# Moving the first sequence's last transposes, and two units of its filter stage, in a Fourier-filter plus SwiGLU kernel

## The chip, the cores and the metric

The kernel runs on one core of a Trainium2 chip. The metric is device microseconds of one execution. Executions are listed as fast or slow; all those used here were fast. The engines are PE (TensorE), VectorE (DVE in the profile), ScalarE (ACT), GpSimd (POOL), and SyncE (SP), which issues most DMAs. "L437" is line 437 of that kernel's own source; the changed kernel is two lines longer, so its later lines differ by one to three.

## The reference, cut to what matters

```python
# x: (8, 3008, 256);  filt_r, filt_i: (1505, 256);  d_ff = 1536
X = np.fft.rfft(x, axis=1)
y = np.fft.irfft(X * (filt_r + 1j * filt_i)[None], n=3008, axis=1)
x = y.reshape(24064, 256)
rms = np.sqrt(np.mean(x * x, axis=-1, keepdims=True) + 1e-06)
xn = x / rms * rms_g
g, val = xn @ w_gate, xn @ w_val
out = (g * sigmoid(g) * val) @ w_out
```

The transform over 3008 = 47 x 64 points is done as two short transforms by matmul, the filter between them, and back. The feed-forward then takes the result in 48 tiles (6 for each of 8 sequences) of 12 slots each. A slot is four gate and value matmuls (`gv`) and four output matmuls (`down`), about 1.3 us of PE. The transforms of the next sequence run between the slots of this one. Only the first sequence has nothing to hide behind: its filter and transposes are a prologue of some 50 us.

## The kernel before

The filter stage of the first sequence. Unit `i` covers two of 32 frequency groups: two matmuls (`b_mm`), two multiplies with the filter (`b_unit`), and the inverse matmuls (`bit_unit`). GpSimd takes four of the units, by way of a copy `v` that ScalarE makes, since the products lie in PSUM, which GpSimd cannot access (the Trainium skill, "Trainium Kernel Development and Optimization", Key Constraints; the trace agrees in that each of its units follows such a copy, of 0.60 us).

```python
eng = nc.vector
if (i in (5, 8, 11, 14)) if b else (i in (3, 7, 10, 13)):
    eng = nc.gpsimd
    v = yp.tile([P, 2, 512], FP32, tag="y", name="v")
    ...
    nc.scalar.activation(out=v, in_=ps, func=AXT.Copy)
    ps = v
eng.tensor_tensor(out=s1, in0=ps, in1=f1, op=ALU.mult)
eng.tensor_tensor(out=s2, in0=ps, in1=f2, op=ALU.mult)
```

`t1_unit(g)` transposes tile `g` of the first transform and evacuates it (VectorE, or ScalarE for `g` 1 and 4). `t2_unit(j, eng, bank)` transposes the `j`-th of twelve pieces after the inverse matmuls; `eng` is 1 for an evacuation by VectorE, 0 for ScalarE. `f_dup` copies half a filter table. `warm_up(n)` and `keep_warm(n)` issue matmuls whose result nobody reads, of 512 and 128 columns; the text calls them dummies. Some lines are joined here, and the comments are added.

```python
t1_unit(0); t1_unit(1)
ps0 = [b_mm(0, i) for i in range(4)]
t1_unit(2); t1_unit(3)
f_dup(0, 0, A)
... # 16 units; then the last inverse blocks
for i in range(12, 16):
    bit_unit(i)
    if i % 2 == 0: keep_warm(4)
warm_up(2, 0)
t2_unit(0, 1); t2_unit(1, 0)
warm_up(2, 0)
first = n_first()          # psn: first tile; squares on ScalarE
warm_up(4, 0)
y_first(*first, 1)
q_unit(0, 0)               # psq; u on VectorE; rho on GpSimd
warm_up(3, 0)
y_first(*first, 0)
scale_split(0, 0)          # hl: rho as two f16 parts, on VectorE
t2_unit(2, 0); t2_unit(3, 0)
warm_up(3, 0)
scale_apply(0, 0, 3)       # psr on PE; xn = y * psr on VectorE
warm_up(1, 0)
t2_unit(4, 0); t2_unit(5, 0)
... # the feed-forward; slots 0 to 5 hold t2_unit(6) to (11)
```

Every later tile but two gets its scale another way. GpSimd computes `rho`, stores it to DRAM (`r_tmp`), SyncE loads it back as a row broadcast to all partitions (`rb`), and GpSimd multiplies: `xn_unit`. The steps are planned by slot:

```python
def norm_plan(b, m, s0, s1, r):
    ...
    steps = (q_unit, rho_load, xn_unit)
    if halved(b, m):                      # late tiles: GpSimd first folds the squares
        at(s1 + 2, fold_unit, b, m)
        r = (4, 8, 11)
    ...
    for d, fn in zip(r, steps):
        at(s1 + d, fn, b, m, ...)
```

In these traces each engine takes up its instructions in program order: in the trace of after, shown below, `hl` waits 1.01 us behind an evacuation although its input is ready.

## Time and profile before

| | before |
|---|---|
| time, median of three | 900.11 us (899.17 to 901.25) |
| span of the profiled execution | 896.9 us |
| PE busy | 877.4 us (98%) |
| first transposes after the inverse (`pt` from `gT`) | 42.37 us |
| first scaling multiply (`xn`) | 48.11 us |
| first output evacuation (`o`, feed-forward tile 0) | 73.57 us |

The page of the profile of before, its busy line and the chain that ended last:

```profile
PE 877.4 (98%) x6307; PEld 563.0 (63%) x6307; DVE 676.7 (75%) x1085; ACT 624.0 (70%) x1063; POOL 427.2 (48%) x384
...
PE 87%; issue 5%; DVE 3%; DMA 2%; POOL 2%; ACT 1%; POOLq 0%; DVEq 0%; ACTq 0%; SPq 0%
```

After the prologue PE is the limit. What a change of the prologue is worth must be read in the prologue's timeline. Three views of before follow, each with start, duration, engine, line, operation and tiles; the bracket is the idle time of the engine before it and what ended it. First VectorE, 18 to 26 us, around the start of the multiplies:

```profile
19.73 0.69 DVE L545 COPY t<-pt 96x1024 f16<-96x1024 f16 x1 [0.75 <-PE pt L543]
22.46 1.29 DVE L545 COPY t<-pt 96x1024 f16<-96x1024 f16 x2 [2.04 <-PE pt L543]
23.66 0.68 DVE L265 TENSOR_TENSOR ss<-psb,fr 128x512 f16<-128x512 f32 x1
```

Then ScalarE in the same time:

```profile
20.25 1.02 ACT L547 ACTIVATE t<-pt 96x1024 f16<-96x1024 f16 x1 [1.70 <-PE pt L543]
21.30 1.94 ACT L510 ACTIVATE fr<-fr 64x2048 f32<-64x2048 f32 x1
```

VectorE idles 2.04 us. The bracket names PE: its transposes of tile 2 (from 21.76 us) stand behind matmuls that need tile 1, which ScalarE evacuates until 21.27. ScalarE then copies the filter half that unit 0 reads, until 23.24. From 23.66 us VectorE multiplies without a gap to 39.88 us. Then the scale chain, all engines, of before:

```profile
42.37 0.86 PE L582 MATMUL pt<-tb,gT 128*128 128x128 f16 x8
...
45.99 1.05 POOL L355 TENSOR_TENSOR rho<-u,mhalf 128x4 f32<-128x4 f32 x1 [1.11 <-DVE u L353]
...
47.08 0.17 DVE L391 CAST hl<-rho 128x4 f16<-128x4 f32 x1 [0.51 <-POOL rho L355]
...
48.11 1.29 DVE L405 TENSOR_TENSOR xn<-psr,y 128x512 f16<-128x512 f32 x2 [0.66 <-PE psr L401]
```

`hl` starts 0.04 us after `rho` ends (45.99 + 1.05 = 47.04): nothing stands between them.

### The profile page before, as it was taken

The page shows a single profiled execution, that of the slowest core. Times are in us where ns is not written, and L with a number is a line of the kernel's source. Part 1 is how long each engine was busy: PE and PEld are TensorE (multiplying, and loading weights), DVE is VectorE, ACT ScalarE, POOL GpSimd, SP SyncE. Part 2 cuts the span into 40 slices and gives each one's busy share as a digit, 9 for nine tenths or more (in the row PEclk, how much of TensorE's full clock was granted, in tenths as well). Part 3 has the DMA queues.
Part 4 walks back from the last instruction along what each step waited for, and adds up shares of the span by engine and source line. Part 5 has one row for each costly group of instructions (what it writes and reads, how often), then busy time and mean ns, then how long its engine had stood idle before and what let it go on. Part 6 is the DMA issues. An engine that isn't in the chain of part 4 may idle for free.

```text
span 896.9 us, 17537 instructions
## 1 busy us (share of the span) xinstructions
PE 877.4 (98%) x6307; PEld 563.0 (63%) x6307; DVE 676.7 (75%) x1085; ACT 624.0 (70%) x1063; POOL 427.2 (48%) x384
## 2 busy tenths in 40 slices
PE   8899999999999999999999999999999999999997
PEld 5666666566666666666666666666666666666556
DVE  6866667788988787888788886887878887555555
ACT  7777666677777766877668766787657765676544
POOL 7842730555635661577326662376515662155300
PEclk9999999999999999999999999999999999999999
DMA  8495725674564337434554347242262232222301
GB/s 200 101 192 169 158 57 185 148 172 103 139 170 115 88 86 202 107 95 114 135 149 105 94 92 196 71 109 82 83 176 72 66 85 56 93 66 48 72 24 48
DMA packets 80094, 101.43 MB, mean 113 GB/s; under 512 B 8108, under 2 KB 56684, under 8 KB 79560
## 3 DMA queue, kind: packets, MB, share of 16 engines
q1 hardware_dynamic: 69688, 84.23, 34.3%
q0 software_dynamic: 10240, 15.96, 11.0%
q8 instruction: 49, 0.80, 0.4%
q14 instruction: 37, 0.30, 0.1%
q10 hardware_dynamic: 80, 0.13, 0.1%
HBM read 67.67 MB, written 46.78 MB: 128 GB/s over the span
## 4 chain that ended last, share of the span: by engine, by line
PE 87%; issue 5%; DVE 3%; DMA 2%; POOL 2%; ACT 1%; POOLq 0%; DVEq 0%; ACTq 0%; SPq 0%
PE po L456 25%; PE pg L437 25%; PE pv L437 25%; PE psi L288 3%; PE psb L238 3%; PE psn L320 2%; PE psa L203 2%; DMA xc<-in_x_dram 1%; DMA rb<-r_tmp 1%; DVE o L463 1%; PE psq L349 1%; DVE hh L442 1%; PE pt L543 0%; POOL xc L188 0%; PE pt L582 0%
## 5 line engine op out<-in xcount | busy, mean ns | idle before, releaser
L442 DVE TENSOR_TENSOR hh<-pv,sg 128x512 f16<-128x512 f32 (+2 forms) x588 | 393.3, 670 | 198.1 <-ACT sg L441 85.8
L441 ACT ACTIVATE sg<-pg 128x512 f16<-128x512 f32 (+2 forms) x588 | 340.8, 580 | 226.5 <-PE pg L437 217.5
L456 PE MATMUL po<-wo,hh 128*128 128x256 f16 x2244 | 342.9, 272 | 2.3 <-DVE o L463 1.6
L437 PE MATMUL pg<-xn,wg 128*128 128x512 f16 (+2 forms) x1176 | 339.5, 370 | 0.2 <-DVE xn L405 0.2
L437 PE MATMUL pv<-xn,wv 128*128 128x512 f16 (+2 forms) x1176 | 339.5, 370 | 0.0
L456 PEld LDWEIGHTS <-hh 128*128 128x128 f16 x2256 | 216.4, 98 | 96.8 <-issue 3.5
L279 POOL TENSOR_TENSOR s<-s,s 128x512 f16<-128x512 f16 x96 | 111.0, 1156 | 230.4 <-DVE s L273 158.3
L437 PEld LDWEIGHTS <-wv 128*128 128x128 f16 x1176 | 114.9, 98 | 129.1 <-issue 0.5
L416 POOL TENSOR_TENSOR xn<-y,rb 128x1024 f16<-128x1024 f32 (+1 forms) x45 | 126.2, 2805 | 42.6 <-DMA rb<-r_tmp 36.2
L437 PEld LDWEIGHTS <-wg 128*128 128x128 f16 x1176 | 111.3, 98 | 12.7 <-issue 0.3
L355 POOL TENSOR_TENSOR rho<-u,mhalf 128x4 f32<-128x4 f32 (+1 forms) x48 | 48.9, 1019 | 68.3 <-DVE u L353 68.0
L293 ACT ACTIVATE t<-psi 96x512 f16<-96x512 f32 x112 | 66.3, 592 | 11.7 <-PE psi L288 6.6
L326 ACT ACTIVATE y<-psn,gsb 128x512 f32<-128x512 f32 (+1 forms) x94 | 63.8, 678 | 9.4 <-PE psn L320 2.4
L273 DVE TENSOR_TENSOR s<-psb,fi 64x512 f16<-64x512 f32 x96 | 65.7, 684 | 3.0
L275 DVE SCALAR_TENSOR_TENSOR s<-psb,fi 64x512 f16<-64x512 f32 x96 | 66.5, 693 | 1.3
L249 DVE TENSOR_TENSOR s<-psb,fr 128x512 f16<-128x512 f32 x96 | 65.4, 681 | 0.0
L340 POOL TENSOR_TENSOR sq<-sq 128x512 f16<-128x512 f16 (+1 forms) x34 | 38.4, 1130 | 36.1 <-ACT sq L332 36.1
L332 ACT ACTIVATE sq<-psn 128x512 f16<-128x512 f32 (+1 forms) x94 | 54.8, 583 | 0.0
L208 ACT ACTIVATE t<-psa 128x512 f16<-128x512 f32 x70 | 41.8, 597 | 5.6 <-PE psa L203 2.4
L288 PE MATMUL psi<-s,wi 128*128 128x256 f16 x248 | 45.4, 273 | 0.0
L238 PE MATMUL psb<-t,wb 96*128 96x256 f16 x224 | 43.0, 272 | 0.9 <-DVE s L266 0.9
L288 PEld LDWEIGHTS <-wi 128*128 128x128 f16 x248 | 24.2, 98 | 27.1 <-issue 2.0
(106 smaller groups left out, 543.7 us busy)
## 6 DMA issues: line engine op xcount, KB each, us to landing
out_dram<-o SPq DMA_DIRECT2D x83, 256.0 KB
xc<-in_x_dram POOLq DMA_DIRECT2D x56, 192.0 KB, 6.0
z_tmp<-t SPq DMA_DIRECT2D x28, 384.0 KB
t<-z_tmp SPq DMA_DIRECT2D x28, 384.0 KB
g_tmp<-t SPq DMA_DIRECT2D x56, 192.0 KB
rb<-r_tmp SPq DMA_DIRECT2D x41, 256.0 KB
t<-g_tmp SPq DMA_DIRECT2D x21, 384.0 KB
t<-g_tmp SPq DMA_DIRECT2D x7, 320.0 KB
```

Source lines behind the costliest of these rows:

```text
L238: nc.tensor.matmul(ps[:, u, :], w[:, k, :], t, start=True, stop=True)
L249: nc.vector.tensor_tensor(out=s1, in0=ps, in1=f1, op=ALU.mult)
L273: nc.vector.tensor_tensor(out=s2[a], in0=ps[e], in1=f2[e], op=ALU.mult)
L275: nc.vector.scalar_tensor_tensor(out=s2[a], in0=ps[e], scalar=-1.0, in1=f2[e], op0=ALU.mult, op1=ALU.mult)
L279: nc.gpsimd.tensor_tensor(out=s, in0=s1, in1=s2, op=ALU.add)
L288: nc.tensor.matmul(ps[:, u, :], wi_at(q, 2 * i + u), ss[q][:, u, :], start=(q == 0), stop=(q == n - 1))
L293: nc.scalar.activation(out=st[b]["t3"][c][:, 2 * r:2 * r + 2, :], in_=ps[0:KR], func=AXT.Copy)
L416: nc.gpsimd.tensor_tensor(out=xv, in0=yv, in1=rv.unsqueeze(1).to_broadcast([P, 2, n, P]), op=ALU.mult)
L437: nc.tensor.matmul(ps[:, 0:w], wt[:, dt_, ts(jt, P)], xn[:, dt_, :], start=(dt_ == 0), stop=(dt_ == 1))
L441: nc.scalar.activation(out=sg[:, 0:w], in_=pg[:, 0:w], func=AXT.Silu)
L442: nc.vector.tensor_tensor(out=hh[:, 0:w], in0=pv[:, 0:w], in1=sg[:, 0:w], op=ALU.mult)
L456: nc.tensor.matmul(po[s4 // per][:, s4 % per, :], hh[:, ts(s4, P)], wo[:, jt, :], start=(jt == 0 and s4 % per == 0), stop=(jt == JT - 1 an ...
```

## The change

It has two intents: to start the filter stage's multiplies sooner by letting VectorE evacuate tile 1, with other units on GpSimd; and to take five of the six remaining transpose units out of the feed-forward's first slots, running them in the scale chain's waits in the place of dummies.

```diff
-        if (i in (5, 8, 11, 14)) if b else (i in (3, 7, 10, 13)):
+        if (i in (5, 8, 11, 14)) if b else (i in (3, 7, 9, 12)):
...
-        if g not in (1, 4):
+        if g not in (3, 4):
...
-        ps0 = [b_mm(0, i) for i in range(4)]
+        ps0 = [b_mm(0, i) for i in range(2)]
         t1_unit(2)
+        ps0 += [b_mm(0, i) for i in range(2, 4)]
+        f_dup(0, 0, A)
         t1_unit(3)
-        f_dup(0, 0, A)
...
             bit_unit(i)
-            if i % 2 == 0:
-                keep_warm(4)
         warm_up(2, 0)
         t2_unit(0, 1)
         t2_unit(1, 0)
-        warm_up(2, 0)
+        t2_unit(2, 1, 0)
         first = n_first()
-        warm_up(4, 0)
+        t2_unit(3, 1, 1)
+        t2_unit(4, 1)
+        t2_unit(5, 1)
+        fill = bank(2, "pw")
+        warm_up(2, fill)
         y_first(*first, 1)
         q_unit(0, 0)
-        warm_up(3, 0)
+        t2_unit(6, 0, 0)
+        t2_unit(7, 0)
+        warm_up(5, fill)
         y_first(*first, 0)
+        t2_unit(8, 1)
         scale_split(0, 0)
-        t2_unit(2, 0)
-        t2_unit(3, 0)
-        warm_up(3, 0)
         scale_apply(0, 0, 3)
-        warm_up(1, 0)
-        t2_unit(4, 0)
-        t2_unit(5, 0)
+        t2_unit(9, 0, 0)
+        t2_unit(10, 0)
...
-        for j in range(6, 12):
-            at(j - 6, t2_unit, j, 1, 1)
+        at(0, t2_unit, 11, 1, 1)
```

(The helper `warm_up` also learns to take a bank; that is cut.)

## The prediction

> **What bounds it now.** The busy table gives PE 877.4 of 896.9 us (98%); the chain that ended last is 87% PE. Only the prologue, before the first feed-forward matmuls (about 49.5 us), has other limits, and every edit lies there. Its timeline shows three stages.
>
> 1. 18.6-41.7 us, filter units. VectorE runs without a gap from 23.66 to 39.88: 12 units of two multiplies (0.60 us apart) plus evacuations. It starts at 23.66 only because ScalarE evacuates tile 1 (20.25, 1.02 us) and then copies the filter half that unit 0 needs (21.30-23.24). At the end PE waits 1.0 us for GpSimd's last unit, 13 (v from ScalarE 37.30, two multiplies of 1.27 us, done 40.44).
> 2. 42.37-49.45 us, the scale chain: transposes, psn, squares, psq, rho (GpSimd 1.05 us), hl, psr, xn. PE fills its waits with 13 dummy 128x512 matmuls, about 0.21 us each.
> 3. 49.5-60 us, first feed-forward slots: each holds one of six transpose units (0.27 us of PE), and PE waits there, e.g. for a VectorE evacuation at 53.1.
>
> **The change.**
> - Tile 1 goes to VectorE, idle 20.4-22.5 us, so the filter copy starts about 2.7 us sooner on ScalarE. Estimate: unit 0 starts near 22.2 us, 1.4 us sooner, limited by tile 2's evacuation.
> - GpSimd gets units 9 and 12 for 10 and 13. Units 3 and 7 still end at 33.3 us (held by filter copies), so 9 runs about 33.2-35.8 and 12 about 36.2-38.8. Four PE blocks of 0.34 us follow 12: transforms end near 40.2 us, not 41.7, and the first transposes start about 1.3 us sooner. The 8 dropped small matmuls lay mostly in waits.
> - The scale chain gets ten transpose units for six, and 9 dummies for 15. But VectorE works in order: three evacuations (0.41 us each) precede u: +0.2 us. Unit 8's transposes follow five dummies (1.07 us), so its evacuation holds hl about 1 us after rho is ready. Estimate: the chain becomes 0.8-1.2 us longer.
> - Five transpose units (5 x 0.27 = 1.35 us of PE) leave the feed-forward slots, and some waits with them: -1.5 us.
>
> Sum: -1.3 + 1.0 - 1.5 = -1.8 us. From slot 7 on PE is at 9 tenths in the slices and its order is unchanged, so the gain should pass to the end whole.
>
> **Prediction: 898.3 us, range 896.4 to 900.3** (8 in 10). Faster by over 2%: 2%; within 2%: 97%; slower: 1%.
>
> **Seen if right.** VectorE's first filter multiply at about 22.2 us; GpSimd's last ends about 38.8; first xn multiply about 6.7 us after the first transposes (5.74 before: 48.11-42.37); hl held by unit 8's evacuation, not by rho; slots 0 to 5 take about 8.3 us, not 9.75; waits after 62 us unchanged.
>
> **What would make it wrong.** If the dummies end sooner, hl is not held and 1 us more is gained. If unit 12 or the filter copies run later, stage 1 gains less. Fewer dummies could cool the PE clock: the Trainium skill, "TensorE: Matmul & The Clock Gate" (Part 4), says transposes do not count as busy for the clock gate; here 48 transposes ran in 3.2 us (66 ns each), close to full speed, and no run shows the gate closing. If it closes, the gain is lost. Weights or the second sequence's x landing late (DMA saturated 43-62 us) would hold PE. The three timings of before span 2 us, the size of the effect.

## The result and the profile after

| | before | after |
|---|---|---|
| time, median (four runs each) | 899.81 us | 899.53 us (897.97 to 899.75) |
| ratio, with 95% interval | | 0.9991 (0.9974 to 1.0008) |
| span of the profiled execution | 896.9 us | 896.2 us |
| PE busy | 877.4 us | 874.3 us |
| first tile evacuation (`t` from `pt`) | 19.73 us | 19.43 us |
| first transposes | 42.37 us | 40.96 us |
| first scaling multiply | 48.11 us | 48.03 us |
| first output evacuation | 73.57 us | 71.86 us |

Ratios here and below are the mean time of one kernel's fast runs over that of the other's of the same rounds, so not quite the ratio of the medians. This one does not tell the two kernels apart. The traces do. VectorE of after, 18 to 26 us:

```profile
19.43 1.28 DVE L545 COPY t<-pt 96x1024 f16<-96x1024 f16 x2 [0.76 <-PE pt L543]
21.28 0.69 DVE L545 COPY t<-pt 96x1024 f16<-96x1024 f16 x1 [0.57 <-PE pt L543]
21.89 0.68 DVE L265 TENSOR_TENSOR ss<-psb,fr 128x512 f16<-128x512 f32 x1
```

The idle 2.04 us is now 0.57, and the first multiply starts at 21.89. The scale chain of after, all engines:

```profile
40.96 1.05 PE L582 MATMUL pt<-tb,gT 128*128 128x128 f16 x12
...
44.66 1.05 POOL L355 TENSOR_TENSOR rho<-u,mhalf 128x4 f32<-128x4 f32 x1 [1.40 <-DVE u L353]
...
44.83 1.24 PE L612 MATMUL pw<-wz 128*128 128x512 f16 x5
...
45.91 0.43 PE L582 MATMUL pt<-tb,gT 128*128 128x128 f16 x4
46.38 0.42 DVE L585 COPY t<-pt 128x512 f16<-128x512 f16 x1 [1.14 <-PE pt L582]
...
46.72 0.45 DVE L391 CAST hl<-rho 128x4 f16<-128x4 f32 x1
...
48.03 1.29 DVE L405 TENSOR_TENSOR xn<-psr,y 128x512 f16<-128x512 f32 x2 [0.66 <-PE psr L401]
```

`rho` ends at 45.71 us but `hl` starts at 46.72: VectorE stood idle for 1.14 us waiting for unit 8's transposes, which PE did behind five dummies, and had to evacuate them first.

To see where the lead goes, align the two traces at every output evacuation on VectorE. There are 49 (numbers 0 to 48), one per tile and one more for the last tile, which is cut in two. Negative means after is ahead:

```
output evacuation     0      2      5      6     11     12     47
before, us        73.57 114.87 169.94 190.16 282.35 301.13 885.71
after - before    -1.71  -1.71  -1.72  -1.50  -1.50  -0.74  -0.73
```

The lead is 1.71 us for the first 100 us of feed-forward, close to the 1.8 predicted, and is lost in two steps, of 0.22 and 0.76 us. After the second it changes by no more than 0.02 us to the end. The second step, GpSimd of before, 281 to 292 us:

```profile
286.62 1.15 POOL L279 TENSOR_TENSOR s<-s,s 128x512 f16<-128x512 f16 x1 [3.98 <-DVE s L273]
287.72 2.87 POOL L416 TENSOR_TENSOR xn<-y,rb 128x1024 f16<-128x1024 f32 x1
290.56 1.15 POOL L340 TENSOR_TENSOR sq<-sq 128x512 f16<-128x512 f16 x1
```

The same three instructions of after:

```profile
285.12 1.15 POOL L279 TENSOR_TENSOR s<-s,s 128x512 f16<-128x512 f16 x1 [3.97 <-DVE s L273]
286.98 2.89 POOL L416 TENSOR_TENSOR xn<-y,rb 128x1024 f16<-128x1024 f32 x1 [0.71 <-DMA rb<-r_tmp]
289.80 1.17 POOL L340 TENSOR_TENSOR sq<-sq 128x512 f16<-128x512 f16 x1
```

SyncE had issued the load of the row that this scaling needs, in before and in after, at:

```profile
281.56 0.34 SPq L364 DMA_DIRECT2D rb<-r_tmp  x1
```

```profile
280.07 0.34 SPq L364 DMA_DIRECT2D rb<-r_tmp  x1
```

The sum comes 1.50 us sooner, and the load of the row, `rb`, is issued 1.49 us sooner; but the row takes longer to land. In after, the scaling waits for it and starts 6.91 us after the issue; in before it starts 6.16 us after the issue and does not wait. So it starts only 0.74 us sooner, and the fold behind it 0.76. PE waits for the fold. In PE's own timeline, of before:

```profile
291.77 0.25 PE L349 MATMUL psq<-ones,sq 128*128 128x1 f16 x4 [0.48 <-POOL sq L340]
```

and of after:

```profile
291.03 0.25 PE L349 MATMUL psq<-ones,sq 128*128 128x1 f16 x4 [1.25 <-POOL sq L340]
```

The wait grew by 0.77 us. The first step, near 174 us, looks alike: GpSimd waits 3.12 us for a row before and 3.36 after, and PE waits behind it 1.68 us before,

```profile
174.63 0.27 PE L288 MATMUL psi<-s,tb 128*128 128x256 f16 x1 [1.68 <-POOL s L279]
```

and 1.91 us after:

```profile
173.13 0.27 PE L288 MATMUL psi<-s,tb 128*128 128x256 f16 x1 [1.91 <-POOL s L279]
```

One pair of traces does not say whether such a step belongs to the change or to the one execution.

### The profile page after: what moved, and what is told of

It reads as the page before. It is cut to its first block, busy times and chain, and to the rows that moved or that the text cites. A ratio compares the mean times of both kernels' runs of the same rounds, so it can differ in the third digit from the quotient of the medians.

```text
span 896.2 us, 17510 instructions
## 1 busy us (share of the span) xinstructions
PE 874.3 (98%) x6293; PEld 561.6 (63%) x6293; DVE 676.9 (76%) x1085; ACT 623.8 (70%) x1063; POOL 427.4 (48%) x384
## 4 chain that ended last, share of the span: by engine, by line
PE 85%; issue 5%; DMA 5%; DVE 3%; POOL 1%; ACT 1%; POOLq 0%; SPq 0%; ACTq 0%
PE po L456 25%; PE pg L437 25%; PE pv L437 24%; PE psi L288 3%; PE psb L238 3%; PE psn L320 2%; DMA fr<-in_filt_r_dram 2%; PE psa L203 2%; DMA rb<-r_tmp 2%; DVE o L463 1%; DVE fr L654 1%; DMA fr<-fr 1%; DVE hh L442 1%; PE psq L349 1%; DMA r_tmp<-rho 0%
```

## The experiments

Twelve kernels ran, all correct against the reference, five rounds each. Kernels of one group shared one chip and its runs of the kernel before. The ratio is to the kernel before of the same rounds, whose median is the last column.

| run | median, us | ratio (95%) | before, us |
|---|---|---|---|
| after_again | 899.53 | 0.9977 (0.9951 to 1.0002) | 901.85 |
| before_fold_first | 902.62 | 1.0005 (0.9979 to 1.0031) | 901.85 |
| after_fold_first | 900.40 | 0.9983 (0.9957 to 1.0009) | 901.85 |
| after_hl_first | 900.73 | 0.9992 (0.9965 to 1.0019) | 901.85 |
| before_slack | 897.34 | 0.9986 (0.9973 to 0.9999) | 898.56 |
| after_slack | 895.65 | 0.9967 (0.9955 to 0.9979) | 898.56 |
| after_slack_hl | 893.95 | 0.9949 (0.9936 to 0.9962) | 898.56 |
| after_slack_nodum | 894.08 | 0.9950 (0.9938 to 0.9962) | 898.56 |
| stage1_slack | 896.31 | 0.9963 (0.9945 to 0.9981) | 899.68 |
| transposes_slack | 895.94 | 0.9962 (0.9942 to 0.9982) | 899.68 |
| after_slack_units_back | 895.31 | 0.9953 (0.9932 to 0.9973) | 899.68 |
| after_slack_hl_nodum | 894.83 | 0.9943 (0.9925 to 0.9961) | 899.68 |

### Group 1: does the wait for scale rows take the lead?

**after_again**: the changed kernel, no edit.

> The changed kernel unedited, for its spread. Theory 1 (the prologue's lead of 1.7 us is given back where GpSimd waits for the landing of a broadcast scale row, because that landing keeps its own time): the lead at the first output evacuation is again 1.6 to 1.8 us, and it falls in steps at the tiles after 170 us and after 282 us, by 0.2 and 0.8 us or more, since landings vary; time ratio 0.998 to 1.0. Rival (the loss is chance of one execution, such as a lower granted clock): steps elsewhere or none, and a slow drift where the clock is below 1.

The times spread from 897.00 to 902.73 us. The profiled execution fell in the slowest, and is the most instructive. Aligned with the first trace of before:

```
output evacuation       0      2      3      5      6     12     47
after_again         -1.39   1.94   2.81   2.82   3.30   3.99   4.00
before_fold_first    0.09   0.13   0.13   0.13   2.44   1.78   1.79
after_fold_first     0.90   3.32   4.16   4.16   4.46   3.98   3.99
after_hl_first      -2.64  -1.89  -1.90  -1.90   0.26   0.67   0.68
```

The lead at evacuation 0 was 1.39 us, below the range expected, with the first tile evacuation at 19.70 us rather than 19.43. The steps at 6 and 12 came again (0.48 and 0.26 us), and one of 0.44 us came at evacuation 10. But a larger loss, 4.2 us in all, came at evacuations 2 and 3, where the theory had nothing. ScalarE of after_again there, around 110 us:

```profile
109.09 0.60 ACT L441 ACTIVATE sg<-pg 128x512 f16<-128x512 f32 x1 [0.70 <-PE pg L437]
113.41 0.59 ACT L293 ACTIVATE t<-psi 96x512 f16<-96x512 f32 x1 [3.73 <-DMA g_tmp<-t]
113.90 0.58 ACT L263 ACTIVATE v<-psb 128x512 f32<-128x512 f32 x1
```

and PE of after_again:

```profile
114.54 0.38 PE L238 MATMUL psb<-t,wb 96*128 96x256 f16 x2 [3.10 <-ACT v L263]
```

ScalarE waits for a store (`g_tmp`) to free its tile. In SyncE's order of issue that store stands behind the load of a scale row, issued at 104.38 us in this run and 103.33 in the first trace of after. So a row can hold PE a second way, through the store behind it. The late row is not all of it: the store was issued at 105.28 us and ScalarE could go on only at 113.41, 8.1 us later, while in the first trace of after ScalarE went on without a wait 5.4 us after the issue (104.23 to 109.65).

**before_fold_first** and **after_fold_first**: one scaling goes to GpSimd a slot later, so that the fold passes it.

```diff
             steps = (q_unit, rho_load, xn_unit)
+            r = {(2, 1): (2, 6, 11)}.get((b, m), r)
```

> The kernel before; the normalization of sequence 2, tile 1 goes to GpSimd one slot later, so that the fold of tile 2's squares passes ahead of it. Theory 1: PE's wait of 0.48 us for the fold (at 291.3 us in the first profile) goes; about 0.5 us less time. Rival: no difference.

> The same edit on the changed kernel. Theory 1: PE's wait of 1.25 us for the fold goes, so 1.2 us less than the changed kernel, and the step of 0.76 us in the lead, taken against the kernel before with the same edit, vanishes: lead about 1.5 us at the end. Rival: the loss moves to another wait and the time stays.

PE's wait for the fold is gone from both traces. From evacuation 11 to 12 both gain 0.66 us on the first trace of before (2.44 to 1.78, and 4.64 to 3.98), where after lost 0.76. So that step is caused by the fold standing behind the row. The expected gains of 0.5 and 1.2 us do not show in the times (intervals of half a percent, about 2.5 us either way), and of the lead of 1.5 us expected at the end nothing is left: after_fold_first ends 2.20 us behind before_fold_first, most of it lost at evacuations 2 and 3. And before_fold_first, which is before in everything up to there, lost 2.31 us against the first trace of before at evacuation 6. Two executions of one kernel can thus differ at that place by more than the lead. A window table of its trace, two microseconds a line, of these columns: window, its length, busy time of PE, weight loads, VectorE, ScalarE and GpSimd, granted TensorE clock, DMA share, GB/s:

```profile
172.00:174.00 2.00, 1.08 (x7) 0.44 (x5) 1.91 (x4) 0.60 (x1) 2.00 (x1) 1.00 0.18 46
174.00:176.00 2.00, 0.47 (x3) 0.34 (x3) 0.55 (x1) 0.00 (x0) 2.00 (x4) 0.82 0.94 238
176.00:178.00 2.00, 2.00 (x8) 0.94 (x7) 0.00 (x0) 0.74 (x2) 1.99 (x3) 0.50 0.82 123
178.00:180.00 2.00, 2.00 (x12) 1.18 (x11) 1.22 (x2) 1.05 (x2) 2.00 (x1) 0.83 0.64 121
```

and PE of the same trace:

```profile
175.53 0.37 PE L288 MATMUL psi<-s,tb 128*128 128x256 f16 x1 [2.45 <-POOL s L279]
...
176.76 1.06 PE L437 MATMUL pg<-xn,wg 128*128 128x512 f16 x2
...
179.46 0.59 PE L437 MATMUL pg<-xn,wg 128*128 128x512 f16 x2
```

A wait of 2.45 us for GpSimd (which waited 3.90 us for its row) was followed by half clock: a pair of gate matmuls took 1.06 us instead of 0.59. The clock lost is 2.00 x (0.18 + 0.50 + 0.17) = 1.70 us. The same sum came out of each of the other dips in the feed-forward of this group: after_hl_first after a wait of 2.16 us at 173, after_again after 3.10 us at 114, after_fold_first after 2.19 us at 116. No dip followed waits of 1.68, 1.91, 1.98 and, once, 2.17 us. The Trainium skill, "TensorE: Matmul & The Clock Gate" (Part 1, What's actually happening), has the mechanism: the clock is halved after an idle window of about 3.4 us, and the window is free-running. A loss of 1.70 us is 3.4 us at half clock, and that 2.16 us once cost it while 2.17 us did not agrees with a window that runs free. That waits shorter than the window were enough is taken up in the last section.

**after_hl_first**: `hl` ahead of unit 8's evacuation.

```diff
-        t2_unit(8, 1)
         scale_split(0, 0)
+        t2_unit(8, 1)
```

> The changed kernel, with the evacuation of transpose unit 8 after the two small hl instructions on VectorE rather than ahead of them. If unit 8's evacuation holds the scale chain as the profile of after says (rho done 45.71, hl started 46.72), hl starts about 45.8 and the first gate matmul about 1.0 us sooner; the lead at the first output evacuation is about 2.7 us. Of this the later waits for scale rows may take some back. Rival (PE's five dummies hold the chain): the gain is below 0.4 us, because psr stands behind dummies and unit 8 on PE.

The chain did what was expected: from first transposes to first scaling took 5.87 us, not 7.07, and the lead at evacuation 0 was 2.64 us. Then 0.75 us went at evacuation 2, 2.16 at 6 (the half clock) and 0.41 at 12, and the time shows nothing (ratio 0.9992, against 0.9977 for the changed kernel in the same rounds).

So the theory needed a second part: rows that land late make PE idle in three places, near 110, 174 and 291 us; and where an idle is long the half clock adds 1.70 us.

### Group 2: the waits for rows taken away from both kernels

The edit moves three scalings to a later slot, and one row load with them. No dependence is removed: GpSimd does the next sum, unit or fold first, and SyncE the store first.

```diff
             steps = (q_unit, rho_load, xn_unit)
+            r = {(0, 5): (2, 9, 13), (1, 1): (2, 5, 9), (2, 1): (2, 6, 11)}.get((b, m), r)
```

**before_slack** and **after_slack**:

> The kernel before, with three normalizations (sequence 0 tile 5, sequence 1 tile 1, sequence 2 tile 1) moved one to five slots later, so that PE no longer depends on when a scale row lands: the row load stands behind the next store on the sync queue, and GpSimd does the next sum, unit or fold ahead of the scaling. Theory 2 (the rows' landing makes PE idle near 110, 174 and 291 us; in executions where one of the idles reaches 2.2 us and more the granted TensorE clock falls to half for about 3.4 us and some 1.7 us more are lost): the waits there go, about 2 us less than before on the profile, granted clock 1.00 between 100 and 190 us, and a narrower spread of times. Rival (the spread comes from elsewhere, such as the first loads): waits move, time and spread stay.

> The same on the changed kernel. Theory 2: the lead over the kernel before with slack, 1.5 to 1.9 us at the first output evacuation less what the first loads happen to do, stays the same at every later output evacuation to 0.1 us; 3 to 5 us less than the kernel before in time. Rival: the lead shrinks again at 170 and 290 us.

GpSimd of before_slack near 170 us shows the new order, the sum no longer behind the row:

```profile
170.09 1.14 POOL L279 TENSOR_TENSOR s<-s,s 128x512 f16<-128x512 f16 x1 [1.92 <-DVE s L273]
171.22 2.88 POOL L416 TENSOR_TENSOR xn<-y,rb 128x1024 f16<-128x1024 f32 x1
```

The waits of PE in the three places are gone in both traces, and the clock is 1.00 from 100 to 190 us. The instruction that had waited near 174 us, in before_slack and in after_slack:

```profile
173.49 0.27 PE L288 MATMUL psi<-s,tb 128*128 128x256 f16 x1
```

```profile
171.51 0.27 PE L288 MATMUL psi<-s,tb 128*128 128x256 f16 x1
```

Aligned with before_slack:

```
output evacuation        0      2      5      6     11     12     47
before_slack, us     74.28 115.58 170.64 189.02 281.20 299.33 883.91
after_slack          -1.98  -1.98  -1.97  -1.98  -1.96  -1.97  -1.97
after_slack_hl       -3.77  -3.77  -3.76  -3.76  -3.75  -3.76  -3.75
after_slack_nodum    -3.40  -3.41  -3.40  -3.40  -3.03  -3.03  -3.03
```

This is the decisive pair: with the rows off the path, the lead stays to 0.02 us through 810 us, where it had lost more than half. The size in this pair, 1.98 us, is 0.6 us too good: before_slack's filter stage had a half-clock dip of its own (granted clock 0.91 between 20 and 40 us), and its first transposes came 23.28 us after the first tile evacuation, not 22.64 as in before. In times, 897.34 and 895.65: the medians differ by 1.7 us. The ratios to before, 0.9986 and 0.9967, give 0.9967 / 0.9986 = 0.9981, or 1.7 us too. The intervals of the two overlap a little. Before with slack gained 1.8 us on the profile (896.9 to 895.1), near the 2 expected, and 1.2 us in the medians; but the spread did not narrow as expected: its six runs span 3.5 us, no less than the kernel before in these rounds (2.6); after_slack gained 2.9, a little under the 3 to 5 expected, and its five runs spread over 1.6. So the rival keeps a part: some of the spread comes from ahead of the feed-forward.

**after_slack_hl** and **after_slack_nodum**: the same, with `hl` ahead of unit 8's evacuation, or without the seven dummies in the chain (`warm_up(2, fill)` and `warm_up(5, fill)` left out).

> As after with slack, and the evacuation of transpose unit 8 behind the hl instructions. With the landings off the path, the about 1 us gained in the scale chain should pass to the end: 0.9 to 1.1 us less than after with slack from the first gate matmul on. Rival (it was given back in the earlier run for another reason): under 0.3 us.

> After with slack, without the seven dummy matmuls between psn and the first scaling. If they still keep the clock up: the granted clock falls below 1.00 between 44 and 52 us, and gate matmuls there take double. If not (the transposes and the short chain suffice): clock 1.00, and the scale chain becomes about 1.0 us shorter, since unit 8's transposes and so its evacuation come 1.07 us sooner and no longer hold hl.

Both remove the hold. VectorE in after_slack_hl:

```profile
45.60 0.17 DVE L391 CAST hl<-rho 128x4 f16<-128x4 f32 x1 [0.51 <-POOL rho L355]
...
46.24 0.42 DVE L585 COPY t<-pt 128x512 f16<-128x512 f16 x1 [0.27 <-PE pt L582]
```

From first transposes to first scaling: 5.87 us with `hl` first and 5.64 without dummies, against 7.07 in after_slack. So 1.2 us of that chain was the evacuation in front of `hl`. What group 1 gave back now reaches the end: the lead over after_slack is 1.79 us at evacuation 0 (of which 0.56 is first loads that happened to land sooner: first tile evacuation 19.25 and 19.81 us) and 1.78 at evacuation 47. The medians fall by 1.7 and 1.6 us. Without dummies the granted clock stayed 1.00 in windows from 40 to 55 us, so in this case they were not needed. Whether that holds when the idle times fall elsewhere in the window, these runs do not show. The 0.37 us that the version without dummies loses at evacuation 10 is a load (`t` from `g_tmp`) that PE's weight load waited for by 0.7 us; and its lead at evacuation 0 is smaller than with `hl` first because its filter half landed later (ScalarE waited 2.31 us for it, and the first multiply 0.55 us for the copy).

### Group 3: the parts alone

**stage1_slack** is before_slack with the filter stage of the change alone, and **transposes_slack** is before_slack with the transposes and dummies of the change alone; stage1_slack keeps the `keep_warm` dummies, transposes_slack drops them.

> The kernel before with slack, and of the change only the filter stage: tile 1 on VectorE, the reordered first units, units 9 and 12 on GpSimd (the dummies after the last inverse blocks are kept). Prediction's sum: the first transposes start about 1.3 us sooner than before with slack, and the lead stays to the end, time 1.0 to 1.5 us less. Rival (the lead of the filter stage comes from a clock dip of the other run): under 0.8 us.

> The kernel before with slack, and of the change only the moved transposes and the dummies. Prediction's sum: the scale chain 0.8 to 1.2 us longer, the first slots 1.5 us shorter: time 0.3 to 0.7 us less than before with slack. Rival (additive sum wrong, the moved transposes do all the good): over 1 us less.

The three durations of each trace, which leave out when the first tile of `x` arrived and what follows. The first of them still depends on when the filter landed: in after_hl_first and after_slack_nodum it is 22.01 and 22.04 us, because the first multiply waited 0.5 us for a filter copy; in the five traces here it did not.

| us | before | stage1_slack | transposes_slack | after | after_slack |
|---|---|---|---|---|---|
| first tile evacuation to first transposes | 22.64 | 21.95 | 22.51 | 21.53 | 21.59 |
| first transposes to first scaling | 5.74 | 5.73 | 7.07 | 7.07 | 7.07 |
| first scaling to output evacuation 0 | 25.46 | 25.47 | 23.83 | 23.83 | 23.83 |

The chain and the slots come out alone as they do together, to 0.01 us: the moved transposes lose 1.33 us in the chain and win 1.63 in the slots, a gain of 0.30 in all, at the low end of the 0.3 to 0.7 expected. The filter stage alone saves 0.69 us against before (1.1 with the small dummies gone, below). Expected were 1.3 us, and under 0.8 for the rival, a clock dip of the other run. That rival holds in part: of the 1.07 us by which stage1_slack leads before_slack to the end, and of the 1.27 of transposes_slack, 0.64 us is before_slack's dip. The missing 0.4 is explained, though not run by itself, by the kept dummies. With unit 12 the last to come from GpSimd, the four blocks after it run back to back, and the two groups of four dummies between them cost 2 x 0.22 us; with unit 13 last, in transposes_slack, one group lay in a wait, and dropping both saved only 0.13. In times, both kernels were about 1.0 to 1.4 us faster than before_slack in medians, but in other rounds; the 1.4 us of transposes_slack lie above the 0.3 to 0.7 expected, and the intervals do not settle which part gives more.

**after_slack_units_back**: GpSimd's units 10 and 13 again.

```diff
-        if (i in (5, 8, 11, 14)) if b else (i in (3, 7, 9, 12)):
+        if (i in (5, 8, 11, 14)) if b else (i in (3, 7, 10, 13)):
```

> After with slack, with GpSimd's units 10 and 13 again. If the choice of units matters for the filter stage: GpSimd's unit 13 ends about 39.5 us, PE's last blocks wait for it, and the first transposes start 0.5 to 0.9 us later than in after with slack. Rival (only tile 1 matters): the first transposes start within 0.2 us of after with slack.

A miss in sign. From first tile evacuation to first transposes took 21.17 us, 0.42 less than in after_slack: the old units are the better ones here. GpSimd's last multiply ended 19.38 us after the first tile evacuation, against 19.46 in after_slack, so the new units free GpSimd no sooner; and behind unit 12 PE still has four blocks to do, of 0.34 us each, behind unit 13 three. All of the filter stage's gain is thus tile 1 and the dropped dummies; the choice of units costs some of it. This is one trace, but the five traces with the new units and the small dummies dropped, without a late filter or a dip, lie between 21.52 and 21.59 us. Not run: the old units together with `hl` first.

**after_slack_hl_nodum**: both remedies for `hl`.

> After with slack, hl ahead of unit 8's evacuation and no dummies in the chain. If each of the two alone only removes the same hold on hl, they do not add: rho to hl is 0.05 us in both, psq comes 0.2 us sooner at most; time within 0.3 us of the hl version. If they add: 1 us less than the hl version.

They do not add, as expected: 5.65 us from first transposes to first scaling, as without dummies alone. This execution lost 1.3 us between the first scaling and evacuation 0 (25.11 us instead of 23.83). GpSimd shows why:

```profile
59.82 0.52 POOL L188 DMA_DIRECT2D xc<-in_x_dram  x1 [4.21 <-DMA wo<-in_moe_w_out_dram]
60.40 1.03 POOL L355 TENSOR_TENSOR rho<-u,mhalf 128x4 f32<-128x4 f32 x1
```

In program order the second tile's `rho` stands behind the issue of the last load of `x`, and that issue waited 4.21 us for an earlier weight load to land; in after_slack_hl the same wait was 1.44 us. PE then waited 0.90 us for the second tile's `hl`. This is the same kind of hold in a fourth place. The median, 894.83 us, is 0.9 us above the hl version's, in other rounds; the expected 0.3 us was missed, but the ratios, 0.9943 and 0.9949, do not tell them apart.

## Why the prediction was right, and where it was not

- **Time.** 899.53 us lies within 896.4 to 900.3, and the predicted 898.3 is 1.2 us off. A right range is cheap here: one execution of the same kernel differs from another by several microseconds. The medians differ by 0.28 us, which is no measured gain; that the range holds the time is in part luck. The sum is tested better by the traces.
- **Filter stage, -1.3 us.** Measured -1.41 at the first transposes (42.37 to 40.96), of which 0.30 is loads that landed sooner in that execution and 1.11 the edits. VectorE's start at 21.89 us is 2.46 us after the first tile evacuation and was 3.93 before: 1.47 sooner, as forecast (1.4). GpSimd ended at 38.83 us, forecast 38.8, and PE's wait before the last blocks was still for it. But crediting GpSimd's new units was wrong: they cost 0.4 us (21.17 us for the stage with the old ones, 21.59 with the new). That the sum still fitted is luck: the dropped small dummies, which the prediction took to lie mostly in waits, were worth about 0.4 us with the new units (21.95 to 21.59) and made up for it.
- **Scale chain, +1.0 us.** Measured +1.33 (5.74 to 7.07). The cause is as told: 1.20 us of it went when `hl` was put ahead of unit 8's evacuation.
- **Slots, -1.5 us.** Measured -1.63 from first scaling to evacuation 0. Slots 0 to 5 took 8.11 us (49.37 to 57.48) for 9.75 before, forecast 8.3.
- **Lead at evacuation 0, -1.8 us.** Measured -1.71, of which 0.30 is the earlier loads: the edits gave -1.11 + 1.33 - 1.63 = -1.41. With slack in both kernels the lead reached the end unchanged.
- **"The gain should pass to the end whole" and "waits after 62 us unchanged": the steps that failed in the traces.** A kernel whose PE is busy 98% and whose order of instructions is unchanged still had three places, 60 to 240 us later, where PE waited for GpSimd or ScalarE, which waited for a DMA. The waits were not unchanged: 1.68 us became 1.91 near 174 us, and 0.48 became 1.25 near 291. The row loads were issued 1.61 and 1.49 us sooner, but from issue to scaling passed 6.98 us for 6.86, and 6.91 for 6.16. In the profiled pair this took back 0.98 of 1.71 us; in another execution of the same kernel 5.4 us went (a lead of 1.39 became a lag of 4.00; 1.70 us of it is half clock). How much of this the change itself causes is not shown: with the old prologue, before_fold_first lost 2.31 us against before at evacuation 6. Nor do the times show the gain lost on average. The changed kernel was 0.8 us faster by the first ratio (0.9991) and 2.1 us by that of after_again (0.9977), and both intervals hold 0 as well as 1.7 us. What the slack pair shows is that these waits are what moves the lead: without them it stays.
- **"Fewer dummies could cool the PE clock".** It did not happen in the scale chain; with no dummies at all in it, the granted clock was 1.00. It happened instead after the long waits, which nobody filled.
- **Open.** Why before's own filter stage shows a half-clock dip in some executions (granted clock 0.93 between 18 and 42 us in two of four traces with the old filter stage, and 0.86 between 18 and 30 us in one of nine with the new one) was not separated, nor how much of the 1.7 us in the medians of the slack pair is due to it. Without a dip the durations above give 1.4 us. What part of the spread of several microseconds comes from the first loads was seen (first tile evacuation from 19.20 to 20.86 us) but not controlled.

The best version is after_slack_hl: 893.95 us, ratio 0.9949 (0.9936 to 0.9962). It is 4.6 us below the kernel before in its rounds. Of that, the change by itself accounts for 1.4 us (by the durations) to 1.7 us (by the medians of the slack pair), about a third.

## What to carry to other kernels

Before crediting a saving ahead of a compute-bound stretch, look in that stretch for engines that do their work in order and have a DMA landing in front of work that PE needs: a landing that varies from execution to execution can take the saving back there. Putting the independent work first kept the lead here. When filling a gap with useful work, check what the filler's evacuation stands in front of on its engine; here one 0.42 us evacuation behind five dummies cost 1.2 us. Align two traces at a repeated event, such as an output evacuation: steps in the difference show where a lead is lost, when the times are too noisy to show that there was one.

## What the Trainium skill lacked or had wrong

- "TensorE: Matmul & The Clock Gate" (Part 1) halves the clock after an idle window of about 3.4 us. Here single PE idles of 2.16, 2.19, 2.45 and 3.10 us were enough, each costing 1.70 us of clock, while 1.68, 1.91, 1.98 and 2.17 us were not. The window that holds them need not be empty: before the dip at 175.5 us PE was busy for 1.08 of the 2.00 us from 172 on. The page does not say how little work in a window counts as idle.
- The same page (Part 4) says transposes do not count as busy for the gate. In the run without dummies in the scale chain, 44 transposes and 24 other small matmuls kept PE busy for 5.19 of the 6.20 us between 41.4 and 47.6 us, and the granted clock stayed 1.00. The trace does not say whether these are in the transpose mode that the page means.
- No page gives the time of a row broadcast from DRAM to all partitions, issued by SyncE, under load; "DMA: Bandwidth & Descriptors" (Anatomy of one DMA — SWDGE (gpsimd) path) gives a fixed cost of about 2.0 us, but for DMAs that GpSimd issues. In before, the 256 KB row took 6.86 us from its issue by SyncE (163.74 us) to the start of the scaling that waited for it (170.60), with the DMA engines 0.86 busy up to 168 us and 0.82 after.
